# Moving one half of a softmax by one slice: batch 3 in slices 4 and 5 of stage 2 in place of 4 and 6

## The chip, the cores and the metric

One core of one Trainium2 chip. The metric is the device time of one execution in microseconds (us). Engines: PE is TensorE, DVE is VectorE, ACT is ScalarE, POOL is GpSimd, SP only issues DMAs here.

## The reference, cut to what matters

```python
def _attn_ref(x, state):                     # x: 8 x 8 x 512 x 64, state: 8 x 8 x 32 x 64
    scores = scale * np.matmul(x, state.transpose(0, 1, 3, 2))
    a = softmax(scores)                      # written out in the original
    xread = np.matmul(a, state)
    scores2 = scale * np.matmul(state, x.transpose(0, 1, 3, 2))
    sread = np.matmul(softmax(scores2), x)
    return np.concatenate([xread, sread], axis=2)

def _moe_ref(x, w_gate, w_val, w_out):       # 4352 rows x 512, d_ff = 1536
    gate = np.maximum(x @ w_gate, 0.0)
    val = x @ w_val
    return gate * val @ w_out
```

## The kernel before

The kernel goes through the eight batches as stages, and through each stage in 12 slices, one for each 128 columns of d_ff. In slice `jf` PE makes the gate and value products (`gv`, four matmuls of 128x128 by 512), ACT applies ReLU (`relu`), VectorE multiplies gate and value (`mult`), and PE does four matmuls of an earlier output product (`out_piece`). In between, the attention of the *next* batch is prepared: two halves of scores and softmax (`att_half`), and U, the product of state and weights, in two blocks of three units (`u_block`). PE writes its products into banks of PSUM (128 x 512 fp32 each); a bank can be written again once the engines that read it have done so. In the traces `sc_ps` are scores, `up` the U units, `sr_ps` the products of sread, `o_ps` output products, and `h_sb` is what the multiply writes.

```python
    def bank(name, kind="r"):
        ...
            n = turn["r"] % 6 if kind == "r" else 6 + turn["o"] % 2    # banks 0 to 5 in turn; 6 and 7 for outputs
            turn[kind] += 1
        return psum.tile([128, 512], FP32, name=name, tag=f"b{n}")

    def u_unit(b, w, lo):
        u_alloc(b)
        ps = held["u", b, w, lo] = [bank("up"), bank("up")]            # two banks for each unit
        u_mm(ps, b, w, lo, 512)                                        # 8 matmuls, the two banks alternating

    def gv(b, jf):
        ...
        held["gv", b, jf] = [bank("gv_ps"), bank("gv_ps")], hsb[b][:, jf], S

    def relu(b, jf):                                                   # ACT reads the gate bank
        ...
    def mult(b, jf):                                                   # VectorE reads the value bank and frees it
        ps, dst, n = held["gv", b, jf]
        nc.vector.tensor_tensor(out=dst, in0=ps[1][:, 0:n], in1=held["g", b, jf][:, 0:n], op=ALU.mult)
    ...
    def att_half(b, kc):
        att_up(b, kc)
        if kc == 1:
            att_aT_dma(b)              # SP: transposing DMA of the softmax's result, ans<-a_sn

    def att_up(b, kc):
        att_sc(b, kc)                  # PE: 8 score matmuls
        att_exp(b, kc)                 # ACT: exp
        att_sum(b, kc)                 # VectorE: row sums and their reciprocal
        att_scale(b, kc)               # VectorE: scaling
    ...
    first, lag = 2 * NF + 4, 18        # this loop starts at slice 4 of stage 2
    at(2, 6, x_dma, 4, (nc.sync,))     # SP: 1 MB load of batch 4's x
    at(2, 8, state_prep, 4, B)         # PE: transposes of the state, stT_ps
    for b in range(3, B):
        s, late = b - 1, 1 if b == 3 else 0
        for i, jf in enumerate((3, 5)):
            at(s, jf + late, att_half, b, i)
        for part, jf in enumerate((7, 10)):
            at(s, jf, u_block, b, part)
            paired.add(NF * s + jf)
        if b + 1 < B:
            at(s, 9, x_next, b + 1)    # POOL: conversion to bf16; SP: transposing DMA, xT<-xb
            at(s, 9, x_pad, b + 1)     # POOL: copy, xa<-xb
        if b + 2 < B:
            at(s, 10, x_dma, b + 2, (nc.sync,))
    ...
    for g in range(first, NF * (B + 1)):
        b, jf = divmod(g, NF)
        gv(b, jf) if b < B else gvs(jf)
        relu(b, jf)
        mult(b, jf)
        if piece <= g - lag:
            out_piece(*divmod(piece, NF))
            piece += 1
        for f in units.get(g, ()):     # att_half, u_block, sr and so on, in the order of the at() calls
            f()
        ...
```

Batch 3 is a special case because the loop starts at slice 4: slice 3 of that stage is in a part written by hand.

The softmax here doesn't subtract the row's maximum and nothing guards it: scores larger than these inputs give would overflow.

Of the kernel before, what the change touches and what calls it, by code (L numbers as in the profile page):

```python
# [16 lines left out]
def kernel(  # L17
# [461 lines left out]
    def at(b, jf, f, *args):  # L479
        units.setdefault(NF * b + jf, []).append(lambda: f(*args))  # L480
# [28 lines left out]
    at(2, 6, x_dma, 4, (nc.sync,))  # L509
    at(2, 8, state_prep, 4, B)  # L510
    for b in range(3, B):
        s, late = b - 1, 1 if b == 3 else 0
        for i, jf in enumerate((3, 5)):
            at(s, jf + late, att_half, b, i)
        for part, jf in enumerate((7, 10)):
            at(s, jf, u_block, b, part)
            paired.add(NF * s + jf)
        if b + 1 < B:
            at(s, 9, x_next, b + 1)
            at(s, 9, x_pad, b + 1)  # L520
        if b + 2 < B:
            at(s, 10, x_dma, b + 2, (nc.sync,))
    for b in range(B):
        s, jf = {0: (2, 3), 1: (2, 4), 2: (2, 7), 3: (2, 10)}.get(b, (b - 1, 10))
# [4 lines left out]
    for g in range(first, NF * (B + 1)):  # L529
        b, jf = divmod(g, NF)  # L530
# [47 lines left out]
```

## Time and profile before

| | before |
|---|---|
| time, median of 3 runs (lowest, highest) | 226.06 us (225.6, 226.16) |
| span of the profiled run | 224.2 us |
| PE busy | 216.0 us, 96% |
| PE's waits for another engine from 62 us to the end | one, shown as 0.5 us |

The head of the page of before: the span, and each engine's busy time.

```profile
span 224.2 us, 4840 instructions
## 1 busy us (share of the span) xinstructions
PE 216.0 (96%) x1937; PEld 106.5 (48%) x1967; DVE 128.9 (57%) x226; ACT 124.9 (56%) x236; POOL 52.8 (24%) x58
```

PE sets the pace, so the question is when PE does nothing. The table of waits of PE in before, from 62 us on: who waited for whom, us in total, how often, the longest.

```profile
engine line waited for: us in total, times, longest us
PE o_ps L353 <- issue: 1.6, 10, 0.2
PE up L291 <- DVE h_sb L344: 0.5, 1, 0.5
```

The issue gaps are ten of 0.16 us. They come where the first of four `o_ps` matmuls is missing from the records (the group is shown as x3), so they are not lost time. One wait is left. Here it is in the timeline of PE in before (start, duration, engine, line, operation, how many, and in brackets idle time and its releaser):

```profile
62.34 0.40 PE L200 MATMUL sc_ps<-stT,xT 128*128 128x64 bf16 x8
...
64.39 0.41 PE L291 MATMUL up<-wg_sb,stT 64*32 64x512 bf16 x8
64.61 0.40 PE L291 MATMUL up<-wv_sb,stT 64*32 64x512 bf16 x8
64.83 0.38 PE L291 MATMUL up<-wg_sb,stT 64*32 64x512 bf16 x1
65.75 0.41 PE L291 MATMUL up<-wg_sb,stT 64*32 64x512 bf16 x7 [0.55 <-DVE h_sb L344]
66.09 0.43 PE L264 MATMUL sr_ps<-xa,e_sn 128*32 128x65 bf16 x32
...
68.19 0.61 PE L129 MATMUL stT_ps<-id,st_b 128*128 128x128 bf16 x8
```

The third unit is broken in two: one matmul goes through, the second must wait. Its bank is the value bank of the same slice's `gv`: two banks of `gv` and six of the U block are eight, and the ring has six. The timeline of DVE in before shows who held that bank:

```profile
61.36 1.48 DVE L344 TENSOR_TENSOR h_sb<-gv_ps,g_sb 128x512 bf16<-128x512 f32 x2
63.40 0.69 DVE L213 TENSOR_REDUCE cs<-e_sn 128x16 f32<-128x512 bf16 x1 [0.56 <-ACT e_sn L207]
64.12 0.25 DVE L215 RECIPROCAL rc<-cs 128x16 f32<-128x16 f32 x1
64.41 0.69 DVE L219 TENSOR_TENSOR a_sn<-e_sn,rc 128x512 bf16<-128x512 bf16 x1
65.02 0.68 DVE L344 TENSOR_TENSOR h_sb<-gv_ps,g_sb 128x512 bf16<-128x512 f32 x1
```

The multiply of slice 7 stands last, behind row sum, reciprocal and scaling of batch 3's second softmax half. It ends at 65.70 us, and PE goes on at 65.75.

### The profile page before, as it was taken

What the parts mean: (1) busy time and instruction counts of PE and PEld (TensorE: products, weight loads), DVE (VectorE), ACT (ScalarE), POOL (GpSimd) and SP (SyncE); (2) the same over time, 40 slices, a digit from 0 to 9 for tenths busy, and PEclk for the clock granted to TensorE, in tenths of its full rate; (3) what the DMA queues carried; (4) which work ended last, traced back from release to release, by engine and by line L of the source; (5) the groups of instructions that cost most, each with busy time, mean ns of one, the idle gap of its engine ahead of it and who ended that gap; (6) DMA issues with size and microseconds to landing.
All of it is one profiled execution on the core that took longest, in us unless ns stands there. A gap on an engine that the chain in (4) does not pass through costs nothing.

```text
span 224.2 us, 4840 instructions
## 1 busy us (share of the span) xinstructions
PE 216.0 (96%) x1937; PEld 106.5 (48%) x1967; DVE 128.9 (57%) x226; ACT 124.9 (56%) x236; POOL 52.8 (24%) x58
## 2 busy tenths in 40 slices
PE   7999999999989999999999999999999999999994
PEld 3644354444444444444444444444444445666543
DVE  3587888667584648673786468646864433222100
ACT  4599877774556744664567456545655444222221
POOL 8889756503306070006000700000000000000000
PEclk9999999999999999999999999999999999999999
DMA  6999999170195931791149113511311111111132
GB/s 148 177 194 197 203 236 284 36 176 3 47 239 111 242 117 47 151 273 50 50 110 261 60 60 102 115 50 47 94 50 47 48 47 50 48 59 75 58 94 94
DMA packets 37799, 25.48 MB, mean 114 GB/s; under 512 B 18864, under 2 KB 33200, under 8 KB 37776
## 3 DMA queue, kind: packets, MB, share of 16 engines
q1 hardware_dynamic: 24912, 16.85, 27.3%
q0 software_dynamic: 11968, 7.47, 21.7%
q10 hardware_dynamic: 896, 0.85, 1.3%
q8 instruction: 15, 0.25, 0.5%
q14 instruction: 8, 0.07, 0.1%
HBM read 18.35 MB, written 8.91 MB: 122 GB/s over the span
## 4 chain that ended last, share of the span: by engine, by line
PE 94%; issue 2%; ACT 2%; DVE 1%; DVEq 0%
PE o_ps L353 37%; PE gv_ps L316 36%; PE gv_ps L333 5%; PE up L291 4%; PE warm_ps L432 3%; PE sc_ps L200 2%; PE upc L291 1%; PE sr_ps L264 1%; PE o_ps L379 1%; ACT U L311 1%; PE aT_ps L235 1%; PE xT_ps L186 1%; ACT e_sn L207 0%; PE stT_ps L129 0%; ACT xT L189 0%
## 5 line engine op out<-in xcount | busy, mean ns | idle before, releaser
L316 PE MATMUL gv_ps<-ans,U 128*128 128x512 bf16 x373 | 93.9, 379 | 0.5
L353 PE MATMUL o_ps<-wo_sb,h_sb 128*128 128x512 bf16 x357 | 91.6, 379 | 2.1 <-issue 1.9
L344 DVE TENSOR_TENSOR h_sb<-gv_ps,g_sb 128x512 bf16<-128x512 f32 x96 | 65.5, 689 | 44.1 <-ACT g_sb L340 42.8
L340 ACT ACTIVATE g_sb<-gv_ps 128x512 bf16<-128x512 f32 (+1 forms) x108 | 62.6, 580 | 48.6 <-PE gv_ps L316 33.8
L316 PEld LDWEIGHTS <-U 128*128 128x128 bf16 x384 | 35.7, 98 | 40.3 <-issue 0.6
L353 PEld LDWEIGHTS <-h_sb 128*128 128x128 bf16 x372 | 35.2, 98 | 39.9 <-issue 1.7
L361 ACT COPY o_sb<-o_ps 128x512 f32<-128x512 f32 x29 | 17.1, 590 | 16.9 <-PE o_ps L353 16.9
L301 ACT CAST U<-up 128x512 bf16<-128x512 f32 x36 | 19.0, 593 | 11.6 <-PE up L291 11.6
L301 DVE CAST U<-up 128x512 bf16<-128x512 f32 x36 | 22.8, 684 | 2.2 <-PE up L291 1.9
L142 POOL CAST xb<-xf 128x1024 bf16<-128x1024 f32 x10 | 10.1, 1042 | 54.1 <-DMA xf<-in_x_dram 34.3
L256 POOL COPY xa<-xb 128x2048 bf16<-128x2048 bf16 (+1 forms) x9 | 15.3, 1713 | 12.2 <-issue 7.3
L213 DVE TENSOR_REDUCE cs<-e_sn 128x16 f32<-128x512 bf16 x16 | 10.9, 684 | 8.4 <-ACT e_sn L207 8.4
L344 DVE TENSOR_TENSOR hs_sb<-gv_ps,g_sb 128x256 bf16<-128x256 f32 x12 | 5.1, 425 | 15.3 <-PE gv_ps L333 10.5
L207 ACT ACTIVATE e_sn<-sc_ps 128x512 bf16<-128x512 f32 x16 | 9.6, 599 | 6.3 <-PE sc_ps L200 6.2
L291 PEld LDWEIGHTS <-stT 64*32 64x32 bf16 x512 | 5.7, 89 | 12.1 <-issue 11.0
L311 ACT CAST U<-upc 128x512 bf16<-128x512 f32 (+1 forms) x20 | 9.5, 533 | 1.4 <-PE upc L291 1.3
L432 PE MATMUL warm_ps<-hs_sb 128*128 128x512 bf16 x20 | 7.8, 507 | 1.4 <-DVE hs_sb L396 1.2
L219 DVE TENSOR_TENSOR a_sn<-e_sn,rc 128x512 bf16<-128x512 bf16 x12 | 8.3, 692 | 0.6
L291 PE MATMUL up<-wg_sb,stT 64*32 64x512 bf16 x144 | 7.7, 382 | 0.5 <-DVE h_sb L344 0.5
L200 PEld LDWEIGHTS <-xT 128*128 128x128 bf16 x128 | 5.7, 98 | 3.8 <-ACT xT L177 0.7
L333 PE MATMUL gv_ps<-br,wg_sb 128*128 128x256 bf16 x48 | 7.2, 273 | 0.1
L333 PE MATMUL gv_ps<-br,wv_sb 128*128 128x256 bf16 x48 | 7.2, 273 | 0.0
(64 smaller groups left out, 130.8 us busy)
## 6 DMA issues: line engine op xcount, KB each, us to landing
out_dram<-o_sb SPq DMA_DIRECT2D x31, 256.0 KB, 2.3
xf<-in_x_dram SPq DMA_DIRECT2D x4, 1024.0 KB, 6.6
wo_sb<-in_moe_w_out_dram POOLq DMA_DIRECT2D x2, 768.0 KB, 14.5
wg_sb<-in_moe_w_gate_dram POOLq DMA_DIRECT2D x5, 256.0 KB, 8.9
wv_sb<-in_moe_w_val_dram POOLq DMA_DIRECT2D x5, 256.0 KB, 9.5
xf<-in_x_dram POOLq DMA_DIRECT2D x1, 1024.0 KB, 15.1
xb<-in_x_dram POOLq DMA_DIRECT2D x3, 256.0 KB, 6.1
xb<-in_x_dram POOLq DMA_DIRECT2D x1, 512.0 KB, 11.4
```

What stands on the lines that cost most here:

```text
L213: nc.vector.reduce_sum(out=cs, in_=e_v, axis=AX.X)
L256: nc.gpsimd.tensor_copy(out=v[:, hs:hs + src.shape[1]], in_=src)
L291: nc.tensor.matmul(dst[parity][32 * j:32 * j + 32], stT[r:r + 64, b, j, 32 * parity:32 * parity + 32], wsb[r:r + 64, j, lo:lo + n], start= ...
L301: copy[eng](out=U[b][:, w, kc, lo:lo + 512], in_=held["u", b, w, lo][kc])
L311: copy[eng](out=U[b][:, :, kc, lo:lo + n], in_=held["c", b, lo][kc])
L316: nc.tensor.matmul(ps[w], U[b][:, w, kc, f0:f0 + 128], ANS[b][:, kc].rearrange("p c t -> p (c t)"), start=(kc == 0), stop=(kc == NK - 1))
L333: nc.tensor.matmul(ps[w][:, 0:nt], wsb[:, j, f0:f0 + 128], br[:, j].rearrange("p b n -> p (b n)"), start=(j == 0), stop=(j == NJ - 1))
L340: nc.scalar.activation(out=g_sb[:, 0:n], in_=ps[0][:, 0:n], func=AF.Relu)
L344: nc.vector.tensor_tensor(out=dst, in0=ps[1][:, 0:n], in1=held["g", b, jf][:, 0:n], op=ALU.mult)
L353: nc.tensor.matmul(held["o", b, tsub], src[:, jf, tsub * 128:(tsub + 1) * 128], wo_sb[:, jf], start=(jf == 0), stop=(jf == NF - 1))
L361: copy[eng](out=o_sb, in_=held["o", b, tsub])
L432: nc.tensor.matmul(warm_ps[:, 0:cols], warm[:, 0:128], warm[:, 0:cols], start=True, stop=True)
```

## The change

The second softmax half of batch 3 goes from slice 6 to slice 5. It is meant to take the softmax's work out of VectorE's queue before the U block of slice 7 needs the bank.

```diff
@@ -509,9 +509,9 @@
     at(2, 6, x_dma, 4, (nc.sync,))
     at(2, 8, state_prep, 4, B)
     for b in range(3, B):
-        s, late = b - 1, 1 if b == 3 else 0
-        for i, jf in enumerate((3, 5)):
-            at(s, jf + late, att_half, b, i)
+        s = b - 1
+        for i, jf in enumerate((4, 5) if b == 3 else (3, 5)):
+            at(s, jf, att_half, b, i)
         for part, jf in enumerate((7, 10)):
             at(s, jf, u_block, b, part)
             paired.add(NF * s + jf)
```

No instruction is added or removed. On PE, ACT and VectorE the pieces of the softmax half move one slice up. On SP the transposing DMA `ans<-a_sn`, formerly behind the 1 MB load of batch 4's x, now stands ahead of it.

## The prediction

> **What bounds the kernel now.** TensorE. The page gives PE 96% busy over a span of 224.2 us; the chain of waits is 94% PE. From 62 us on, PE's wait table holds one wait for another engine: the `up` matmuls for the VectorE product `h_sb` (the last gated multiply), shown as 0.5 us at 65.75 us; the rest is issue gaps of 0.2 us. It falls in slice 7 of stage 2, in batch 3's first U block. After it PE runs back to back, so time lost there reaches the end.
>
> **Where that wait comes from.** The U block takes six PSUM banks; the sixth is the value bank of the slice's own gv product, which the multiply of slice 7 frees. On VectorE that multiply stands behind the softmax of batch 3's second half (row sum 0.69, reciprocal 0.25, scaling 0.69 us), issued in slice 6. In the timeline the row sum starts at 63.40, the multiply at 65.02, ending 65.70; PE goes on at 65.75. The Trainium skill, "PSUM — Partial Sum Buffer", section Engine vs sequencer instructions, calls the VectorE queue strictly first in, first out; the trace agrees. The wait table understates the loss: the third `up` group started at 64.83 and should have run on about 0.03 us later (a group of 8 takes 0.22 us). From the block's first `up` to the next `o_ps` matmul it is 2.29 us, but 1.36 us in slice 10 with the same work: an estimated 0.9 us lost.
>
> **What changes.** No work is added or removed. On PE eight score matmuls come one slice earlier; on ACT the exp moves ahead of a small copy and a ReLU; on VectorE the softmax ahead of slice 6's multiply; on the SP queue the transposing DMA of batch 3's weights ahead of the 1 MB load of batch 4's x. No bank that PE needs soon is freed late.
>
> **Estimate.** VectorE, with durations as now: row sum 62.0, scaling 63.0 to 63.7, multiply of slice 6 at 63.6, of slice 7 at 64.25 to 64.95. PE goes on at about 65.0 in place of 65.75, against 64.86 with no wait: 0.75 us gained, 0.1 left, all on the critical path.
>
> **The risk.** The load of batch 4's x is now issued behind the transposing DMA, which waits for the scaling: 65.1 in place of 61.8 us. It took 7.2 us to land; others took 5.9 to 6.9. So it lands near 72 in place of 69; its conversion on POOL (2.03 us) and its transposing DMA (6.2 us in this stage, 4.4 later) end near 78 to 80.4; the scores that read it come at about 81.2. The slack falls from 4.5 us to 1 to 3: no stall, probably.
>
> **Predicted time:** 225.3 us (226.06 less 0.75), 8 in 10 between 224.8 and 225.9. Faster by over 2%: 0.005; within 2%: 0.985; slower: 0.01.
>
> **What would show it.** Right: PE's wait for `h_sb` at 65 us is under 0.2 us; 2.29 us in slice 7 become about 1.5; the end comes 0.75 us earlier; x lands later but the score matmuls near 81.2 us do not wait. Wrong: a new PE wait in slices 5 to 7, or PE waiting for xT near 81 us.
>
> **What would make it wrong.** ACT late with exp (it stands behind an output copy); the x load landing over 2 us later than I think; run-to-run scatter (225.6 to 226.16 before), nearly as large as the gain.

## The result, and the profile after

| | before | after |
|---|---|---|
| median of 6 runs each (lowest, highest) | 226.06 us (225.46, 226.23) | 225.51 us (225.02, 226.23) |
| ratio | | 0.9981, 95% interval 0.996 to 1.0003 |
| span of the profiled run | 224.2 us | 223.9 us |

Ratios here and below are the mean time of one kernel's fast runs over that of the other's in the same rounds, so they are not quite the ratio of the medians. The first comparison leaves open whether there is a gain; the repeats below settle that.

The table of waits of PE after, from 62 us on; the wait for `h_sb` is gone:

```profile
engine line waited for: us in total, times, longest us
PE o_ps L353 <- issue: 1.6, 10, 0.2
```

The timeline of PE after. The U block's three units stand back to back:

```profile
61.04 0.40 PE L200 MATMUL sc_ps<-stT,xT 128*128 128x64 bf16 x8
...
64.87 0.41 PE L291 MATMUL up<-wg_sb,stT 64*32 64x512 bf16 x8
65.10 0.40 PE L291 MATMUL up<-wv_sb,stT 64*32 64x512 bf16 x8
65.32 0.47 PE L291 MATMUL up<-wg_sb,stT 64*32 64x512 bf16 x8
65.72 0.43 PE L264 MATMUL sr_ps<-xa,e_sn 128*32 128x65 bf16 x32
...
67.82 0.61 PE L129 MATMUL stT_ps<-id,st_b 128*128 128x128 bf16 x8
```

The timeline of DVE after. The softmax half now lies between the multiplies of slices 5 and 6, and the last two multiplies end at 65.33 us:

```profile
61.84 0.68 DVE L344 TENSOR_TENSOR h_sb<-gv_ps,g_sb 128x512 bf16<-128x512 f32 x1
62.44 0.68 DVE L213 TENSOR_REDUCE cs<-e_sn 128x16 f32<-128x512 bf16 x1
63.15 0.25 DVE L215 RECIPROCAL rc<-cs 128x16 f32<-128x16 f32 x1
63.44 0.69 DVE L219 TENSOR_TENSOR a_sn<-e_sn,rc 128x512 bf16<-128x512 bf16 x1
64.05 1.28 DVE L344 TENSOR_TENSOR h_sb<-gv_ps,g_sb 128x512 bf16<-128x512 f32 x2
```

Absolute times mislead here: this trace reached stage 2 later than that of before. So I cut each span in three, at two points of PE's timeline: the `sr_ps` matmuls of batch 1, just ahead of slice 4 (56.44 us in before, 56.92 after), and the state transposes `stT_ps` of slice 8 (68.19 and 67.82). The *lead* comes before, the *stretch* lies between, the *tail* follows. The order of instructions in the lead is the same in all kernels.

| | lead | stretch | tail | span |
|---|---|---|---|---|
| before | 56.44 | 11.75 | 156.01 | 224.2 |
| after | 56.92 | 10.90 | 156.08 | 223.9 |

The stretch got 0.85 us shorter. The lead happened to be 0.48 us longer in this execution, and took over half of it back.

### The profile page after: what moved, and what is told of

Same layout as the page of the kernel before. It is cut to its first block, busy times and chain, and to the rows that moved or that the text cites. A ratio compares the mean times of both kernels' runs of the same rounds, so it can differ in the third digit from the quotient of the medians.

```text
span 223.9 us, 4840 instructions
## 1 busy us (share of the span) xinstructions
PE 215.5 (96%) x1937; PEld 105.8 (47%) x1967; DVE 129.0 (58%) x226; ACT 124.8 (56%) x236; POOL 53.0 (24%) x58
## 4 chain that ended last, share of the span: by engine, by line
PE 84%; DMA 9%; POOL 4%; issue 2%; DVE 0%; POOLq 0%; DVEq 0%
PE o_ps L353 38%; PE gv_ps L316 31%; DMA xb<-in_x_dram 9%; PE gv_ps L333 5%; PE up L291 4%; PE sr_ps L264 1%; POOL wv_sb L110 1%; PE sc_ps L200 1%; PE o_ps L379 1%; POOL wg_sb L110 1%; POOL a_sn L219 1%; PE xT_ps L186 0%; POOL xb L412 0%; PE stT_ps L129 0%; POOL xb L420 0%
## 5 line engine op out<-in xcount | busy, mean ns | idle before, releaser
L432 PE MATMUL warm_ps<-hs_sb 128*128 128x512 bf16 x20 | 7.2, 470 | 1.4 <-DVE hs_sb L396 1.2
```

## The experiments

The main theory: the multiply of slice 7 no longer stands behind a softmax half on VectorE, so PE's sixth U bank is free in time. Rivals: (A) only the 0.5 us of the wait table was to be had; (B) nothing, start-up scatter; (C) an earlier transposing DMA, or the changed order of loads, does it. Twelve kernels ran (two of them the change itself, unedited), in three groups of four, each group on one chip with its own runs of before; all gave correct results. Two further ideas, batch 3's first half in slice 3, did not build, since the loop never reaches that slice.

The stretch, lead and tail of each run are read from the timeline of PE as above; "U to sr" is the time from the first `up` matmul of slice 7 to the following `sr_ps` matmuls. All in us. "Long scaling" is explained under the second question.

| kernel | lead | stretch | tail | U to sr | time ratio to before, 95% interval | long scaling in stage 3 |
|---|---|---|---|---|---|---|
| before | 56.44 | 11.75 | 156.01 | 1.70 | | 0.69 |
| after | 56.92 | 10.90 | 156.08 | 0.85 | 0.9981 (0.996 to 1.0003) | 0.91 |
| r_after | 56.33 | 10.90 | 156.07 | 0.84 | 0.9974 (0.9961 to 0.9986) | 1.05 |
| e_sp_order | 55.88 | 10.90 | 156.62 | 0.84 | 0.997 (0.9958 to 0.9982) | 2.26 |
| e_third_late | 55.76 | 11.05 | 156.09 | (moved) | 0.9969 (0.9954 to 0.9983) | 0.76 |
| e_pool_scale | 56.48 | 10.99 | 156.03 | 0.92 | 0.9975 (0.996 to 0.999) | 1.70 |
| e_dose1 | 56.26 | 11.49 | 156.05 | 1.44 | 0.9989 (0.9963 to 1.0015) | 0.99 |
| e_dose2 | 56.68 | 12.09 | 156.53 | 2.03 | 1.0032 (1.0003 to 1.0062) | 2.21 |
| e_56 | 55.79 | 12.34 | 156.07 | 2.28 | 1.0018 (0.999 to 1.0046) | 0.69 |
| e_x_late | 56.28 | 10.90 | 156.12 | 0.85 | 0.9976 (0.9943 to 1.0008) | 0.69 |
| r_after2 | 55.81 | 10.91 | 155.98 | 0.84 | 0.9955 (0.994 to 0.9971) | 0.95 |
| e_x5_early | 55.89 | 10.90 | 156.01 | 0.84 | 0.9963 (0.9945 to 0.9981) | 0.69 |
| e_sp_x5 | 56.06 | 10.91 | 156.03 | 0.84 | 0.9962 (0.9945 to 0.9978) | 0.69 |
| e_before_x5 | 56.14 | 11.76 | 156.00 | 1.70 | 1.0003 (0.9986 to 1.0019) | 0.69 |

### First question: what gives the 0.85 us?

**r_after**, the change again, unedited, 5 rounds.

> The change again, beside before on one chip. The stretch from the sr_ps matmuls of batch 1 (56.44 us in before) to the state transposes of slice 8 (68.19) is 11.75 us in before. Theory (the multiply of slice 7 no longer stands behind a softmax half, so PE's sixth U bank is free in time): 10.9 us, first up to next o_ps 1.44 us, time 0.7 to 0.9 us under before. Rival A (the 0.5 us of the wait table is all there was): 0.5 us under. Rival B (nothing, start-up scatter): time within 0.2 us of before.

Measured: medians 225.07 us against 225.67; stretch 10.90 us. The interval excludes 1, so rival B falls. Rival A falls by the stretch: 0.85 us, not 0.5. The mean gain in time, 0.6 us, would by itself allow either.

**e_sp_order**, the change with SP's old order.

```diff
-    at(2, 6, x_dma, 4, (nc.sync,))
+    at(2, 5, x_dma, 4, (nc.sync,))
```

> The change, but with the 1 MB load of batch 4's x issued ahead of batch 3's transposing DMA, as in before. Theory: the stretch stays 10.9 us and the time equals r_after within 0.2 us; the load lands near 69 us. Rival C (the gain comes from the earlier transposing DMA, or a part of it is lost to the later load): the gain falls to 0.3 us or less, or grows by 0.2 us or more.

Measured: load of x issued at 61.25 us, ahead of the transposing DMA at 63.16. Stretch 10.90 us, median 225.06 us, as r_after's 225.07. The order on SP gives nothing of the gain. (Its tail is 0.6 us long; see the second question.)

**e_third_late**: before, with only the third U unit of slice 7 issued later; the softmax stays in slices 4 and 6.

```diff
-        for w, lo in ((0, 0), (1, 0), (0, 512), (1, 512), (0, 1024), (1, 1024))[3 * part:3 * part + 3]:
+        lo3, hi3 = (3 * part, 3 * part + 3) if (b, part) != (3, 0) else (0, 2)
+        for w, lo in ((0, 0), (1, 0), (0, 512), (1, 512), (0, 1024), (1, 1024))[lo3:hi3]:
...
             out_piece(*divmod(piece, NF))
             piece += 1
+        if g == 2 * NF + 7:
+            u_unit(3, 0, 512)
+            u_out(3, 0, 512, 0, "act")
+            u_out(3, 0, 512, 1, "dve")
```

> Before, with the softmax left in slices 4 and 6; only the third U unit of slice 7 is issued after the slice's extra output piece, about 1.5 us of PE work later. Theory: the multiply still ends near 65.7 us, but nobody waits for it any more; the stretch falls to about 10.9 us and the time equals r_after within 0.2 us. Rival C (an earlier softmax or transposing DMA is what pays): no gain over before.

The third unit in the timeline of PE, in one piece and without a wait:

```profile
65.60 0.41 PE L291 MATMUL up<-wg_sb,stT 64*32 64x512 bf16 x8
```

Measured: the multiply started at 64.34 us behind the scaling, as in before, and the third unit at 65.60. Stretch 11.05 us, median 225.06 us. Gain without any move of the softmax or of a DMA: rival C falls. The 0.15 us above 10.90 looks like the price of issuing the unit alone (from the start of the output piece to the unit 0.97 us pass, where four such matmuls take 0.86 elsewhere).

**e_pool_scale**: before, with one scaling on POOL.

```diff
-        att_scale(b, kc)
+        att_scale(b, kc, "pool" if (b, kc) == (3, 1) else "dve")
```

> Before, with the scaling of batch 3's second half on POOL, which is idle there, in place of VectorE. Theory (VectorE's queue order): the multiply starts near 64.4 us in place of 65.02 and ends near 65.1; PE goes on near 65.15; first up to next o_ps falls from 2.29 to about 1.7 us; the stretch is about 11.15 us, the time 0.6 us under before. If the wait is for the softmax's result and not for VectorE's turn, it stays at 2.29 us or grows (POOL takes 1.05 us for this scaling).

The multiply of slice 7 on DVE, and the scaling on POOL:

```profile
64.34 0.63 DVE L344 TENSOR_TENSOR h_sb<-gv_ps,g_sb 128x512 bf16<-128x512 f32 x1
...
64.57 1.05 POOL L219 TENSOR_TENSOR a_sn<-e_sn,rc 128x512 bf16<-128x512 bf16 x1 [5.59 <-DVE rc L215]
```

Measured: the scaling ran on POOL from 64.57 to 65.62 us, the multiply started at 64.34 behind the reciprocal alone; U to sr 0.92 us, stretch 10.99. PE does not wait for the softmax's result (that came later than before), but for VectorE's turn. The gain in the stretch, 0.76 us, is larger than the 0.6 us expected, mostly because the multiply ended at 64.97 us and not near 65.1. ACT's queue, which the change also reorders, stands here as in before: its order is not needed for the gain.

**e_dose1** and **e_dose2**: the change, with one or two superfluous row sums on VectorE ahead of the multiply of slice 7.

```diff
+    def extra():
+        for _ in range(1):                       # 2 in e_dose2
+            cs = small.tile([128, 2 * NC, 2], FP32, name="cs", tag="cs")
+            nc.vector.reduce_sum(out=cs, in_=by_pair(e_sn[3], 1).rearrange("p r (j n) -> p r j n", n=Ns), axis=AX.X)
+
     first, lag = 2 * NF + 4, 18
+    at(2, 6, extra)
     at(2, 6, x_dma, 4, (nc.sync,))
```

> The change, plus one superfluous row sum (0.69 us) on VectorE between the multiplies of slices 6 and 7. Theory: after the change VectorE has no slack left there (the multiply ended at 65.33 us, PE's third U group began at 65.32), so all of it comes back as PE wait: first up to next o_ps 1.44 plus about 0.65, so 2.1 us; the stretch 11.55 us. If there were slack, or the place of the softmax counted and not VectorE's backlog, it would stay at 1.44.

> As e_dose1 with two superfluous row sums. Theory: PE loses about 1.3 us: first up to next o_ps 2.75 us, the stretch 12.2 us; a straight line through r_after, e_dose1 and e_dose2 with a slope of one PE us to one VectorE us.

The same place in the timeline of PE in e_dose1:

```profile
64.65 0.38 PE L291 MATMUL up<-wg_sb,stT 64*32 64x512 bf16 x1
65.31 0.41 PE L291 MATMUL up<-wg_sb,stT 64*32 64x512 bf16 x7 [0.28 <-DVE h_sb L344]
```

and in e_dose2:

```profile
65.08 0.38 PE L291 MATMUL up<-wg_sb,stT 64*32 64x512 bf16 x1
66.33 0.41 PE L291 MATMUL up<-wg_sb,stT 64*32 64x512 bf16 x7 [0.87 <-DVE h_sb L344]
```

Measured: the stretch grew by 0.59 us with one row sum and 1.19 with two. That is the straight line, with no slack left after the change, at 0.60 us a row sum in place of my 0.65. The timeline of DVE in e_dose1 says why:

```profile
63.99 0.68 DVE L511 TENSOR_REDUCE cs<-e_sn 128x16 f32<-128x512 bf16 x1
64.58 0.68 DVE L344 TENSOR_TENSOR h_sb<-gv_ps,g_sb 128x512 bf16<-128x512 f32 x1
```

A row sum is *shown* with 0.68 us, but the next instruction *starts* 0.59 us after it. What this row sum cost the queue is the distance of the starts. (The Trainium skill, "Perfetto Trace Analysis", section DVE / Act Engine Instruction, says that the shown window ends with the acknowledged write, while the next instruction may begin its prefetch before that; the overlap of 0.09 us agrees.)

The two brackets teach a second thing. PE lost 0.59 and 1.19 us, but the wait is shown as 0.28 and 0.87; in before 0.85 against 0.55. Against the change, the shown wait is short by about 0.31 us each time. It is counted from the *end* of the lone matmul, shown with 0.38 us, while in an unbroken unit the next one starts about 0.03 us later (eight in 0.22 us). The same page, section Tensor Engine Instruction, says that matmul ends in a profile are estimated. So I read the loss from starts here.

**e_56**: the halves adjacent, but one slice later.

```diff
-        for i, jf in enumerate((4, 5) if b == 3 else (3, 5)):
+        for i, jf in enumerate((5, 6) if b == 3 else (3, 5)):
```

> Softmax halves of batch 3 in slices 5 and 6: adjacent as in the change, but the second half still in slice 6 as in before, and the first one slice nearer. Theory (VectorE's backlog at the multiply of slice 7): worse than before, first up to next o_ps near 3.0 us, the stretch near 12.45 us, time 0.7 us over before. If adjacency or the earlier start of a half were what pays, it would be no worse than before.

Measured: stretch 12.34 us, 0.59 more than before and 1.44 more than the change. The expected 3.0 us to `o_ps` was 2.65 in the trace (63.74 to 66.39), 0.22 of the difference because the first `o_ps` record is there in this trace and missing in before (from `sr_ps` to the first shown `o_ps` 0.37 us against 0.59). Adjacency is not what pays. The time ratio, 1.0018, leaves open by itself whether it is slower.

### Second question: is any of it given back later?

The prediction named a risk: x of batch 4 is loaded later, and so is everything behind it. SP's timeline of before:

```profile
61.80 0.39 SPq L104 DMA_DIRECT2D xf<-in_x_dram  x1
65.17 1.76 SPq L227 DMA_TRANSPOSE ans<-a_sn  x1
...
71.14 1.93 SPq L159 DMA_TRANSPOSE xT<-xb  x1
73.16 0.94 SPq L104 DMA_DIRECT2D xf<-in_x_dram  x1
```

and after:

```profile
64.19 1.24 SPq L227 DMA_TRANSPOSE ans<-a_sn  x1
65.53 0.53 SPq L104 DMA_DIRECT2D xf<-in_x_dram  x1
...
73.40 2.71 SPq L159 DMA_TRANSPOSE xT<-xb  x1
76.21 0.54 SPq L104 DMA_DIRECT2D xf<-in_x_dram  x1
```

The load is issued 3.7 us later, but batch 4's transposing DMA only 2.3 us later: POOL could start converting 5.8 us after the issue (71.35 us) in place of 7.3. The `ans` transfer no longer falls into the load; in e_sp_order, where it does, the same distance was 8.1 us (61.25 to 69.35). Over all traces it is 5.45 to 6.43 us in the seven where the `ans` transfer goes ahead of the load, and 7.07 to 8.10 in the seven where it does not. The transposing DMA then took 4.3 us, to 77.7; the score matmuls that read xT start at 81.71. The slack is 4.0 us, 4.7 in before.

**e_x_late**: the change, with that load behind one more output store.

```diff
-    at(2, 6, x_dma, 4, (nc.sync,))
+    at(2, 8, x_dma, 4, (nc.sync,))
```

> The change, with the load of batch 4's x issued one output store later still (near 68.1 us in place of 65.5). It tests the risk term: the load landed 5.8 us after its issue in the change and the transposing DMA 4.3 us after its own, so xT should be there near 80.4 us, ahead of the score matmuls at 81.7: no PE wait, time as the change. If the slack in the change was only the 1 us of the low end of the prediction, PE waits over 1 us for xT near 81.7 us.

Measured: load issued at 67.52 us, transposing DMA at 76.00 and landed 4.4 us later, at 80.4; the score matmuls started at 81.07 without a wait; stretch 10.90 us and tail 156.12. So even with 0.7 us of slack nothing is lost: the risk was there, but smaller than I put it.

There is another effect, which the prediction did not see. Lines of DVE and POOL in the timeline of before, stage 3, around the softmax of batch 4's first half:

```profile
82.17 1.90 POOL L256 COPY xa<-xb 128x2048 bf16<-128x2048 bf16 x1
...
84.29 0.69 DVE L219 TENSOR_TENSOR a_sn<-e_sn,rc 128x512 bf16<-128x512 bf16 x1
```

after:

```profile
82.26 2.02 POOL L142 CAST xb<-xf 128x1024 bf16<-128x1024 f32 x2 [6.92 <-DMA xf<-in_x_dram]
...
83.92 0.91 DVE L219 TENSOR_TENSOR a_sn<-e_sn,rc 128x512 bf16<-128x512 bf16 x1
...
84.35 2.24 POOL L256 COPY xa<-xb 128x2048 bf16<-128x2048 bf16 x1
```

and in e_sp_order:

```profile
82.70 1.90 POOL L256 COPY xa<-xb 128x2048 bf16<-128x2048 bf16 x1
82.87 2.26 DVE L219 TENSOR_TENSOR a_sn<-e_sn,rc 128x512 bf16<-128x512 bf16 x1
```

In before POOL is done at 84.07 us and VectorE's scaling starts 0.22 us later, with 0.69 us. After, POOL's work on batch 5's x comes about 2 us later and the softmax a little earlier (0.37 us in this pair of traces), so the scaling starts inside a POOL instruction and is shown as longer. Each long one ends 0.54 us or so after the POOL instruction it ran into: 84.83 against 84.28 after, 84.37 against 83.83 in r_after, 85.13 against 84.60 in e_sp_order. The Trainium skill, "SBUF — State Buffer", section SBUF: two separate sides, says that a VectorE instruction with two SBUF inputs and a GpSimd instruction that reads SBUF contend for a shared port pair, an exclusive lock: whichever starts first holds it for the whole instruction, and the other fully blocks. These ends agree with it, and so does POOL's copy after, which began during the scaling and took 2.24 us in place of 1.90. So does the row sum, which has one input: it ran beside the same POOL conversion at 82.77 us and took its usual 0.69. In the 14 traces this scaling overlaps a POOL conversion or copy in eight and is long in those eight; in the other six it takes 0.69 us. (In e_x_late POOL's conversion came so late, at 85.26 us, that it met the second half's scaling instead: 0.74 us, ending 0.53 after the conversion.) That the overlap does it is shown; that it is the port, and nothing else that the two engines share, rests on the page.

The later load is not needed for the collision. In e_third_late the loads kept their place, and POOL's copy ended 27.37 us after the end of the lead, even before the 27.63 of before; but PE's gain brought the scaling forward from 27.85 to 27.15, and it still ran into the copy.

Mostly this costs nothing: in stage 3 PE waited in no trace where the scaling took 1.70 us or less. At 2.26 (e_sp_order) and 2.21 us (e_dose2) VectorE was still behind when the U block of slice 7 of *stage 3* came, and the tail grew by about 0.55 us. The table of waits of PE in e_sp_order, from 68 us on:

```profile
engine line waited for: us in total, times, longest us
PE up L291 <- DVE h_sb L344: 0.2, 1, 0.2
```

It is the same wait at the same place as the one that the change took away, one stage later. I tested this with the load of batch 5's x issued earlier, so that POOL has converted it before that softmax.

**r_after2**, the change a third time, beside the next three.

> The change a third time, on one chip with the next three. Five of the seven traces of kernels without the wait in slice 7 show something new in stage 3: the scaling of batch 4's first half on VectorE (0.69 us in before) runs into POOL's conversion or copy of batch 5's x and lasts 0.76 to 2.26 us; in one of them PE then lost 0.57 us in slice 7 of stage 3. Theory D ([...] POOL's work comes about 2 us later since the x loads do): this scaling lasts over 0.69 us again and ends about 0.54 us after the POOL instruction it ran into. Stretch of stage 2 10.90 us; time 0.5 to 0.9 us under before.

(The count in this text is off: there were six traces of kernels without the wait, and five of them show the long scaling.) Measured: scaling 0.95 us, ending at 83.76 us, 0.54 after POOL's conversion at 83.22; stretch 10.91 us; medians 224.73 us against 225.76, a gain of 1.03.

**e_x5_early**, the change with the earlier load; **e_sp_x5**, e_sp_order with it; **e_before_x5**, before with it. The same edit in all three:

```diff
         if b + 2 < B:
-            at(s, 10, x_dma, b + 2, (nc.sync,))
+            at(s, 8 if b == 3 else 10, x_dma, b + 2, (nc.sync,))
```

> The change, with the load of batch 5's x issued ahead of batch 4's transposing DMA, so that POOL converts it near 77 to 81 us, before batch 4's softmax. Theory D: the scaling of batch 4's first half is 0.69 us again, no PE wait in stage 3, stretch of stage 2 still 10.90 us; time 0.85 us under before, 0 to 0.25 us under r_after2. If batch 5's work on POOL is not the cause, the scaling stays long in this trace.

> e_sp_order with the early load of batch 5. Its trace had the longest scaling (2.26 us) and the 0.57 us PE loss in slice 7 of stage 3. Theory D: scaling 0.69 us, no PE wait in stage 3, from stage 2's state transposes to the end 156.05 us (156.6 in e_sp_order). Otherwise the loss may come again.

> Before, with only the early load of batch 5's x. Theory: nothing to gain, the 0.9 us loss in slice 7 of stage 2 stays (first up to the next sr_ps matmuls 1.70 us), the time within 0.2 us of before. If the later loads (not VectorE's order) decided the whole change, this kernel would gain as well.

The lines of e_sp_x5 that answer to those of e_sp_order above:

```profile
73.81 2.03 POOL L142 CAST xb<-xf 128x1024 bf16<-128x1024 f32 x2 [1.22 <-DMA xf<-in_x_dram]
...
75.89 1.90 POOL L256 COPY xa<-xb 128x2048 bf16<-128x2048 bf16 x1
...
83.06 0.69 DVE L219 TENSOR_TENSOR a_sn<-e_sn,rc 128x512 bf16<-128x512 bf16 x1
```

Measured: with POOL done by 77.8 to 78.7 us the scaling is 0.69 us in all three. In e_sp_x5 the tail is 156.03 us in place of 156.62 and PE's wait in stage 3 is gone. e_before_x5 keeps its loss in slice 7 (1.70 us) and does not gain (225.9 us against 225.76). So the collision is the cause of the long scaling, and it is no part of the change's gain. In time e_x5_early (224.9 us) is not better than r_after2 (224.73 us): in these executions the change seldom pays for the collision, or too little to be seen. How often an execution loses the 0.55 us is open; of the ten traces of altered kernels without the early load two show it, and neither is of the change itself. No kernel tried is measurably faster than the change.

## Why the prediction was right

- **The wait and its cause: right.** The multiply of slice 7 held the bank. Three independent ways to get it out of PE's way (softmax earlier, U unit later, scaling on POOL) gave 0.85, 0.70 and 0.76 us of stretch, and more work ahead of it cost 0.60 us for each row sum.
- **The size: right, slightly low.** Predicted 0.75 us gained and 0.1 left; the stretch got 0.85 us shorter, and U to sr is 0.85 us, against 0.77 in slice 10 (71.87 to 72.64 us after), so 0.08 is left. Set on before's clock (0.48 us less), row sum, scaling and end of the multiply came at 61.96, 62.96 and 64.85 us; predicted were 62.0, 63.0 and 64.95.
- **The reading that the wait table understates the loss: right.** It showed 0.55 us of 0.85.
- **The time: right, with luck in it.** Predicted 225.3 us, measured 225.51. Over the three comparisons the medians differ by 0.55, 0.60 and 1.03 us. The lead alone ran from 55.76 to 56.92 us over the traces, with the same instructions in the same order, so a gain of 0.85 us is of the size of the scatter of one execution; and the range given, up to 225.9 us, would have held a gain of 0.2 us as well. Where it shows up cleanly is the stretch.
- **The risk: of the right kind, its size wrong.** Predicted slack at xT 1 to 3 us; measured 4.0. The terms that were mis-sized are the load (5.8 us to the start of the conversion in place of about 7, with the transposing DMA out of its way) and batch 4's transposing DMA (4.3 us; the prediction allowed 4.4 to 6.2).
- **Missed:** that POOL's work on batch 5's x would run into a VectorE instruction in stage 3. It lengthened that instruction in each trace of the change by 0.2 to 0.4 us without reaching PE; in e_sp_order, a variant, it cost about 0.55 us.

## What to carry to other kernels

When PE waits for a PSUM bank, ask which instruction frees the bank and what stands ahead of it in that engine's queue; here any one of three moves was enough: issue the work ahead earlier, give a part of it to another engine, or let PE need the bank later. Measure gains below the scatter of the time by the distance between two fixed points of the timeline, and count starts, not shown ends. A reordering, and the gain itself, moves work of the other engines against each other: look one stage on for what now coincides.

## What the Trainium skill lacked or had wrong

- "SBUF — State Buffer" states the exclusive lock, and the traces agree; it does not say what a blocked instruction looks like in a profile. Here it appears as a longer instruction, not as a wait: the VectorE scaling of 0.69 us was shown with up to 2.26 us, and ended about 0.54 us after the POOL instruction did (0.15 less than an unblocked scaling takes; why is open).
- "Perfetto Trace Analysis" says that matmul ends are estimated; it does not give the consequence for waits. With small pipelined matmuls (eight in 0.22 us, each shown with 0.38) the shown idle time was about 0.31 us short of the loss: 0.28, 0.55, 0.87 and 1.13 us shown for 0.59, 0.85, 1.19 and 1.44 us lost against the change.
- No page warns that a profile can lack the first matmul of a group and then show a gap of 0.16 us as waiting for issue, ten times from 62 us on in both main traces.
